# Row sums of squares from half as many matmuls after an add on GpSimd, and the last block in two halves, in a spectral filter with a SwiGLU layer

## The chip, the core and the metric

The kernel runs on one core of a Trainium2 chip. TensorE (PE in the profile) multiplies matrices; VectorE (DVE), ScalarE (ACT) and GpSimd (POOL) do elementwise work, each with its own queue of instructions, worked off in order; SyncE (SP) issues most of the DMA transfers, and GpSimd issues the rest. The metric is the time of one execution on the device, in microseconds.

## What is computed

The input x holds 8 sequences of 3008 rows with 256 channels. Each channel of each sequence is filtered in the frequency domain; every row of the result then goes through an RMS norm and a SwiGLU layer of width 1536.

```
X = rfft(x, axis=1)
y = irfft(X * (filt_r + 1j * filt_i), n=3008, axis=1)      # 8 x 3008 x 256
r = sqrt(mean(y * y, over the 256 channels) + 1e-6)
n = y / r * rms_g
out = (silu(n @ w_gate) * (n @ w_val)) @ w_out
```

The part of interest is the mean of the squares: one number for each of the 24064 rows, over 256 channels.

## The kernel before

The sequences are numbered b = 0 to 7. The layer works through blocks of 512 rows, m = 0 to 5 for each sequence (the last block of an even sequence has three quarters of 128 rows, 384; that of an odd one carries the even one's remaining rows along). The 1536 hidden channels come in JT = 12 slices, jt. One triple (b, m, jt) is an item, and the loop at the end of the program takes one item per slot. For item i it emits, in this order:

- `pre` work planned for the slot (second halves of the filter products, `swap_unit`),
- `gv` (L410): four matmuls of 512 columns, two into `pg` and two into `pv`; ScalarE's silu of `pg` into `sg` (L424); VectorE's product of `pv` and `sg` into `hh` (L425),
- `plan` work (everything else that prepares later blocks and sequences),
- `down` (L428) of item i-2: four matmuls of 256 columns that add to `po0` and `po1` (L437); on the last slice ScalarE copies `po0` and VectorE `po1` into `o3` (L442, L443),
- `late` work (`q_unit`), then, if due, `o_store`: two DMA issues on SyncE, three for the last block of an odd sequence (L452, L456).

`pg` and `pv` have two buffers each; `po0`, `po1` and `mx` have one.

A block is prepared some ten to twenty slots ahead of its first use, in these steps:

- `n_unit`, once for each half of the channels, dh = 0 and 1 (L318): four matmuls into `psn`; ScalarE writes y times the gain (L324) and, a slot later, the squares `sq`, fp16, 128 partitions by 512 rows for each half (`sq_unit`, L330). The partitions are the channels of the half.
- `q_unit` (L339): for every quarter of 128 rows and each half, one matmul with the quarter of `sq` as weights and a column of ones, so that the sums over channels come out as one column per quarter, `psq`. The second half is added in PSUM. VectorE makes `u` = sum/256 + eps (L343), GpSimd `rho` = u to the power -1/2 (L345), and GpSimd issues the DMA that writes it to DRAM (`r_tmp`, L347). `psq` takes one of the two `pg` buffers.
- `rho_load` (L354): SyncE issues a DMA that spreads the block's values over all partitions, `rb`.
- `xn_unit` (L403): GpSimd multiplies y by `rb` into `xn`, the block's operand in `gv`.

The slots are written out by hand. With t = 72(b-1) for sequence b from 2 on, block m's second `n_unit` stands at slot s1 = t + 55 + 8m (in sequence 2, where t is 72, at t + 59 + 8m), its `sq_unit` at s1 + 1, and q_unit, rho_load and xn_unit at s1 + 2, s1 + 6 and s1 + 10. Block m of sequence b is first used at slot 72b + 12m. While these run, the next sequence goes through its filter: `b_unit` (psb, L241 and L247), `swap_unit` (L271, L273), the add on GpSimd (L277), `bi_unit` (psi, L286), with one of each every four slots; `x_load` (L189) is issued on GpSimd's queue, and `z_store`, `t2_load`, `g_store`, `t4_load` on SyncE's. All work planned for one slot is emitted in the order in which it was planned: earlier sequences first, and in a sequence earlier blocks first.

Of the kernel before, what the change touches and what calls it, by code (L numbers as in the profile page):

```python
# [22 lines left out]
B = 8  # L23
DFF = 1536
JT = DFF // P
H = 24
# [96 lines left out]
def kernel(  # L123
# [33 lines left out]
    psO = ctx.enter_context(tc.tile_pool(name="psO", bufs=1, space=bass.MemoryType.PSUM))  # L157
    psM = ctx.enter_context(tc.tile_pool(name="psM", bufs=1, space=bass.MemoryType.PSUM))
# [11 lines left out]
    wo = glob.tile([P, JT, D], FP16)  # L170
    gsb = glob.tile([P, 2], FP32)
    hhs = [glob.tile([P, 512], FP16, name="hh%d" % i) for i in range(4)]
# [4 lines left out]
    st = {b: {"x": {}, "t1": {}, "t2": {}, "s": {}, "t3": {}, "t4": {}, "y": {}, "sq": {},  # L177
              "u": {}, "xn": {}} for b in range(B)}
# [13 lines left out]
    def bank(i, name):  # L192

        pool, tag = ((psM, "mx"), (psG, "pg"), (psV, "pv"), (psB, "mb"), (psO, "po1"), (psO, "po0"))[i]
        return pool.tile([P, 512], FP32, tag=tag, name=name)
# [111 lines left out]
    def nq(b, m):  # L307
        return 3 if (m == 5 and b % 2 == 0) else 4
# [19 lines left out]
    def sq_unit(b, m, dh):  # L328
        w = nq(b, m) * P
        nc.scalar.activation(out=st[b]["sq"][m][:, dh, 0:w], in_=st[b]["sq"].pop((m, dh))[:, 0:w],  # L330
                             func=AXT.Square)

    def q_unit(b, m):
        sq = st[b]["sq"].pop(m)
        ps = bank(1, "psq")
        n = nq(b, m)
        for q in range(n):
            for dh in range(2):
                nc.tensor.matmul(ps[:, q:q + 1], sq[:, dh, ts(q, P)], ones,  # L339
                                 start=(dh == 0), stop=(dh == 1))  # L340
        u = up.tile([P, 4], FP32, tag="u", name="u")
        rho = up.tile([P, 4], FP32, tag="rho", name="rho")
        nc.vector.tensor_scalar(out=u[:, 0:n], in0=ps[:, 0:n], scalar1=1.0 / D, scalar2=1e-6 * Y_SCALE * Y_SCALE,  # L343
                                op0=ALU.mult, op1=ALU.add)
        nc.gpsimd.tensor_tensor(out=rho[:, 0:n], in0=u[:, 0:n], in1=mhalf[:, 0:n], op=ALU.pow)  # L345
        if (b, m) not in by_matmul:
            nc.gpsimd.dma_start(r_d[b, m, 0:n * P].rearrange("(p q) -> p q", q=n), rho[:, 0:n])  # L347
        else:
            st[b]["u"][m] = rho
# [59 lines left out]
    hh_of = {}  # L409
    po_of = {}  # L410
    late_p = {}

    def gv(b, m, jt):
        w = nq(b, m) * P
        xn = st[b]["xn"][m]
        pg = psG.tile([P, 512], FP32, tag="pg", name="pg")
        pv = psV.tile([P, 512], FP32, tag="pv", name="pv")
        for ps, wt in ((pg, wg), (pv, wv)):
            for dt_ in range(2):
                nc.tensor.matmul(ps[:, 0:w], wt[:, dt_, ts(jt, P)], xn[:, dt_, 0:w],  # L420
                                 start=(dt_ == 0), stop=(dt_ == 1))
        sg = hp.tile([P, 512], FP16, tag="sg", name="sg")
        hh = hhs[(6 * JT * b + JT * m + jt) % 4]
        nc.scalar.activation(out=sg[:, 0:w], in_=pg[:, 0:w], func=AXT.Silu)  # L424
        nc.vector.tensor_tensor(out=hh[:, 0:w], in0=pv[:, 0:w], in1=sg[:, 0:w], op=ALU.mult)  # L425
        hh_of[(b, m, jt)] = hh

    def down(b, m, jt):  # L428
        hh = hh_of.pop((b, m, jt))
        if jt == 0:  # L430
            po_of[(b, m)] = [psO.tile([P, 2, D], FP32, tag="po%d" % i, name="po%d" % i)
                             for i in range(2)]
        po = po_of[(b, m)]

        n = nq(b, m)
        for s4 in range(n):
            nc.tensor.matmul(po[s4 // 2][:, s4 % 2, :], hh[:, ts(s4, P)], wo[:, jt, :],  # L437
                             start=(jt == 0 and s4 % 2 == 0),
                             stop=(jt == JT - 1 and (s4 % 2 == 1 or s4 == n - 1)))
        if jt == JT - 1:  # L440
            o3 = late_p["op"].tile([P, 4, D], FP32, tag="o3", name="o3")
            nc.scalar.activation(out=o3[:, 0:2, :], in_=po[0], func=AXT.Copy)  # L442
            nc.vector.tensor_copy(out=o3[:, 2:n, :], in_=po[1][:, 0:n - 2, :])  # L443
            po_of[(b, m)] = o3

    def o_store(b, m):
        o3 = po_of.pop((b, m))
        rows = out[b * N:(b + 1) * N, :].rearrange("(n2 n1) d -> n2 n1 d", n1=N1)
        for h in range(2):
            w = 3 if (m == 5 and (h or b % 2 == 0)) else 4  # L450
            lo = h * H + 4 * m
            nc.sync.dma_start(rows[:, lo:lo + w, :], o3[h * 64:h * 64 + 64, 0:w, :])  # L452
        if m == 5 and b % 2:

            prev = out[(b - 1) * N:b * N, :].rearrange("(n2 n1) d -> n2 n1 d", n1=N1)
            nc.sync.dma_start(prev[:, H - 1, :], o3[64:P, 3, :])  # L456
# [129 lines left out]
    with tc.manual_schedule():  # L586
# [65 lines left out]
        warm_up(2, 0)  # L652
        first = n_first()
        q_unit(0, 0)
        y_first(*first, 0)
        scale_split(0, 0)
# [24 lines left out]
            for name in ("sp", "ssp"):  # L681
                late_p[name] = ctx.enter_context(tc.tile_pool(name=name, bufs=3))

        items = [(b, m, jt) for b in range(B) for m in range(6) for jt in range(JT)]
        pre, plan, late = {}, {}, {}

        def at(slot, fn, *a):
            todo = {q_unit: late, swap_unit: pre}.get(fn, plan).setdefault(slot, [])
            if fn == sq_unit:
                todo.insert(0, (fn, a))  # L690
            else:
                todo.append((fn, a))

        def norm_plan(b, m, s0, s1, r):
            for dh in range(2):
                at((s0, s1)[dh], n_unit, b, m, dh)
                at((s0, s1)[dh] + 1, sq_unit, b, m, dh)
            steps = (q_unit, rho_load, xn_unit)
            if (b, m) in by_matmul:
                steps = (q_unit, scale_split, scale_apply)  # L700
            for d, fn in zip(r, steps):
                at(s1 + d, fn, b, m, *((3,) if fn == scale_apply else ()))

        for j in range(6, 12):
            at(j - 6, t2_unit, j, 1, 1)
        norm_plan(0, 1, 0, 2, (2, 4, 6))
        at(6, open_late)
        at(20, open_sp)
        for m, s0 in ((2, 4), (3, 15), (4, 19), (5, 23)):
            norm_plan(0, m, s0, s0 + 2, (2, 5, 8))  # L710
        for b in range(1, B):
# [42 lines left out]
            for m in range(6):  # L754
                step = 2 if b == 1 and m < 3 else n_step
                norm_plan(b, m, n_at[m], n_at[m] + step,
                          (2, 6, 10) if b > 1 else (2, 5, 8))

        stores = {}
        for i in range(len(items) + 4):  # L760
            for fn, a in pre.get(i, ()):
                fn(*a)
            if i < len(items):
                gv(*items[i])
            for fn, a in plan.get(i, ()):
                fn(*a)
            if 2 <= i < len(items) + 2:
                down(*items[i - 2])
                if items[i - 2][2] == JT - 1:
                    stores[i + 1] = items[i - 2][:2]  # L770
            for fn, a in late.get(i, ()):
                fn(*a)
            if i in stores:
                o_store(*stores[i])
# [30 lines left out]
```

## Time and profile before

| | |
|---|---|
| time, median of 4 runs | 906.89 us (904.4 to 907.7) |
| the profiled execution | 904.1 us, span 902.3 us, TensorE clock 0.99 |
| GpSimd, s add (L277), 128x512 fp16 | 96 of them, 1152 ns each |
| GpSimd, xn (L403) | 45, 2.80 us on the mean |
| GpSimd, rho (L345) | 48, 1.02 us on the mean |
| VectorE, hh (L425), 512 and 384 columns | 692 and 557 ns |
| ScalarE, sg (L424), 512 and 384 columns | 597 and 492 ns |
| psq matmuls (L339) | 376, with as many weight loads |
| r_tmp, from issue to landing | 1.8 us |
| x load, from issue to landing | 6.3 us |
| output store (L452), two issues | 1.11 us on SyncE, 512 KB |

The page gives, for each engine, busy time, its share of the span and the number of instructions. A group's line gives the line of the program, engine, operation and tiles, the count, busy time and mean length of one, and what ended the idle time ahead of it. The lengths of matmuls are those of one alone; they overlap, so that the distance between starts tells what one costs. A timeline merges neighbouring instructions of one group into a line with a count.

### The profile page before, as it was taken

The numbers are of one execution on the slowest core, as the hardware profiler recorded it, in microseconds if no ns is written. First come the engines' busy times: TensorE is split into PE (matmuls) and PEld (weight loads), VectorE is DVE, ScalarE is ACT, GpSimd is POOL, SyncE is SP. The second block draws the span as 40 slices with busy tenths as digits, with TensorE's granted clock in tenths as the row PEclk, the third lists the DMA queues.
The fourth block names the chain that finished last, engine by engine and source line by source line (L and its number), as shares of the span: only waits on it lengthen the run. The fifth ranks groups of instructions, "written<-read, shape, count | busy, mean of one in ns | idle before, by whom it ended". The sixth has DMA issues, their size and how long they took to land.

```text
span 902.3 us, 17520 instructions
## 1 busy us (share of the span) xinstructions
PE 880.3 (98%) x6329; PEld 561.8 (62%) x6329; DVE 677.1 (75%) x1075; ACT 619.5 (69%) x1047; POOL 391.6 (43%) x353
## 2 busy tenths in 40 slices
PE   8799999999999999999999999999999999999997
PEld 5565666666666666766666666666666666666554
DVE  8766767788987787888788886888878887555554
ACT  8667666677777766877667766787657765676443
POOL 8842730555635552465325552265514552043300
PEclk9699999999999999999999999999999999999999
DMA  9495725674564437434554247332252232321201
GB/s 201 83 182 167 155 56 176 158 172 86 154 176 108 98 73 204 106 95 118 136 144 109 88 98 195 83 100 82 77 170 72 64 88 55 99 69 48 60 24 46
DMA packets 79746, 100.91 MB, mean 112 GB/s; under 512 B 8096, under 2 KB 56416, under 8 KB 79276
## 3 DMA queue, kind: packets, MB, share of 16 engines
q1 hardware_dynamic: 69276, 83.45, 33.0%
q0 software_dynamic: 10384, 16.35, 11.2%
q8 instruction: 49, 0.80, 0.4%
q14 instruction: 37, 0.30, 0.1%
HBM read 67.67 MB, written 46.78 MB: 127 GB/s over the span
## 4 chain that ended last, share of the span: by engine, by line
PE 86%; issue 5%; DMA 3%; DVE 3%; ACT 1%; POOL 1%; SPq 0%; POOLq 0%; ACTq 0%; DVEq 0%
PE po L437 25%; PE pg L420 25%; PE pv L420 25%; PE psb L241 3%; PE psi L286 3%; PE psn L318 2%; PE psa L204 2%; DMA fr<-in_filt_r_dram 1%; PE psq L339 1%; DVE o L443 1%; DMA rb<-r_tmp 1%; DMA g_tmp<-t 1%; DVE fr L614 1%; ACT sg L424 0%; DVE hh L425 0%
## 5 line engine op out<-in xcount | busy, mean ns | idle before, releaser
L425 DVE TENSOR_TENSOR hh<-pv,sg 128x512 f16<-128x512 f32 (+1 forms) x576 | 391.5, 680 | 203.6 <-ACT sg L424 88.8
L424 ACT ACTIVATE sg<-pg 128x512 f16<-128x512 f32 (+1 forms) x576 | 338.9, 588 | 230.8 <-PE pg L420 222.9
L437 PE MATMUL po<-wo,hh 128*128 128x256 f16 x2256 | 342.2, 272 | 2.3 <-DVE o L443 1.6
L420 PE MATMUL pv<-xn,wv 128*128 128x512 f16 (+1 forms) x1152 | 337.9, 375 | 0.0
L420 PE MATMUL pg<-xn,wg 128*128 128x512 f16 (+1 forms) x1152 | 337.8, 375 | 0.0
L437 PEld LDWEIGHTS <-hh 128*128 128x128 f16 x2256 | 216.5, 98 | 99.2 <-issue 3.6
L277 POOL TENSOR_TENSOR s<-s,s 128x512 f16<-128x512 f16 x96 | 110.6, 1152 | 285.4 <-DVE s L271 207.3
L420 PEld LDWEIGHTS <-wv 128*128 128x128 f16 x1152 | 112.6, 98 | 131.3 <-issue 0.6
L403 POOL TENSOR_TENSOR xn<-y,rb 128x1024 f16<-128x1024 f32 (+1 forms) x45 | 126.0, 2799 | 45.5 <-DMA rb<-r_tmp 32.1
L420 PEld LDWEIGHTS <-wg 128*128 128x128 f16 x1152 | 109.1, 98 | 12.3 <-issue 0.3
L345 POOL TENSOR_TENSOR rho<-u,mhalf 128x4 f32<-128x4 f32 (+1 forms) x48 | 48.9, 1019 | 84.8 <-DVE u L343 84.8
L291 ACT ACTIVATE t<-psi 96x512 f16<-96x512 f32 x112 | 66.4, 593 | 12.3 <-PE psi L286 6.4
L324 ACT ACTIVATE y<-psn,gsb 128x512 f32<-128x512 f32 (+1 forms) x94 | 63.8, 679 | 9.7 <-PE psn L318 2.6
L271 DVE TENSOR_TENSOR s<-psb,fi 64x512 f16<-64x512 f32 x96 | 65.7, 685 | 3.0
L273 DVE SCALAR_TENSOR_TENSOR s<-psb,fi 64x512 f16<-64x512 f32 x96 | 66.5, 693 | 1.3
L247 DVE TENSOR_TENSOR s<-psb,fr 128x512 f16<-128x512 f32 x96 | 65.4, 681 | 0.0
L330 ACT ACTIVATE sq<-psn 128x512 f16<-128x512 f32 (+1 forms) x94 | 54.7, 582 | 0.0
L209 ACT ACTIVATE t<-psa 128x512 f16<-128x512 f32 x70 | 41.8, 597 | 5.6 <-PE psa L204 2.4
L286 PE MATMUL psi<-s,wi 128*128 128x256 f16 x248 | 45.4, 273 | 0.0
L241 PE MATMUL psb<-t,wb 96*128 96x256 f16 x224 | 43.0, 272 | 1.2 <-DVE s L264 0.9
L286 PEld LDWEIGHTS <-wi 128*128 128x128 f16 x248 | 24.2, 98 | 27.1 <-issue 2.0
L318 PEld LDWEIGHTS <-t 128*128 128x128 f16 x368 | 28.3, 98 | 19.9
(97 smaller groups left out, 519.1 us busy)
## 6 DMA issues: line engine op xcount, KB each, us to landing
out_dram<-o SPq DMA_DIRECT2D x84, 256.0 KB
xc<-in_x_dram POOLq DMA_DIRECT2D x56, 192.0 KB, 6.3
z_tmp<-t SPq DMA_DIRECT2D x28, 384.0 KB
t<-z_tmp SPq DMA_DIRECT2D x28, 384.0 KB
g_tmp<-t SPq DMA_DIRECT2D x56, 192.0 KB
rb<-r_tmp SPq DMA_DIRECT2D x41, 256.0 KB
t<-g_tmp SPq DMA_DIRECT2D x21, 384.0 KB
out_dram<-o SPq DMA_DIRECT2D x12, 192.0 KB
```

The lines of the kernel that those rows point to most:

```text
L241: nc.tensor.matmul(ps[:, u, :], w[:, k, :], t, start=True, stop=True)
L247: nc.vector.tensor_tensor(out=s1, in0=ps, in1=f1, op=ALU.mult)
L271: nc.vector.tensor_tensor(out=s2[a], in0=ps[e], in1=f2[e], op=ALU.mult)
L273: nc.vector.scalar_tensor_tensor(out=s2[a], in0=ps[e], scalar=-1.0, in1=f2[e], op0=ALU.mult, op1=ALU.mult)
L277: nc.gpsimd.tensor_tensor(out=s, in0=s1, in1=s2, op=ALU.add)
L286: nc.tensor.matmul(ps[:, u, :], wi_at(q, 2 * i + u), ss[q][:, u, :], start=(q == 0), stop=(q == n - 1))
L291: nc.scalar.activation(out=st[b]["t3"][c][:, 2 * r:2 * r + 2, :], in_=ps[0:KR], func=AXT.Copy)
L403: nc.gpsimd.tensor_tensor(out=xv, in0=yv, in1=rv.unsqueeze(1).to_broadcast([P, 2, n, P]), op=ALU.mult)
L420: nc.tensor.matmul(ps[:, 0:w], wt[:, dt_, ts(jt, P)], xn[:, dt_, 0:w], start=(dt_ == 0), stop=(dt_ == 1))
L424: nc.scalar.activation(out=sg[:, 0:w], in_=pg[:, 0:w], func=AXT.Silu)
L425: nc.vector.tensor_tensor(out=hh[:, 0:w], in0=pv[:, 0:w], in1=sg[:, 0:w], op=ALU.mult)
L437: nc.tensor.matmul(po[s4 // 2][:, s4 % 2, :], hh[:, ts(s4, P)], wo[:, jt, :], start=(jt == 0 and s4 % 2 == 0), stop=(jt == JT - 1 and (s4 ...
```

## The change

There are two parts. In the first, for blocks 2 to 5 of sequence 2 and all blocks of sequences 3 to 7, `fold_unit` on GpSimd adds the two halves of `sq` in place, at slot s1 + 2, and `q_unit` multiplies by the ones once per quarter. For these blocks q_unit, rho_load and xn_unit stand at s1 + 4, s1 + 8 and s1 + 11.

In the second, the last block of the last sequence (b = 7, m = 5) is cut into two parts of 256 rows with 12 items each. The first part adds up in `po0`, the second in `po1` and `mx`, one quarter in each. ScalarE and VectorE copy one quarter each. The stores of the second part are two issues on SyncE and one on ScalarE's queue; those of the first are two on SyncE.

```diff
+    def halved(b, m):
+        return b > 2 or (b == 2 and m > 1)
+
+    def fold_unit(b, m):
+        sq, w = st[b]["sq"][m], nq(b, m) * P
+        nc.gpsimd.tensor_tensor(out=sq[:, 0, 0:w], in0=sq[:, 0, 0:w], in1=sq[:, 1, 0:w], op=ALU.add)
+
     def q_unit(b, m):
...
+        parts = 1 if halved(b, m) else 2
         for q in range(n):
-            for dh in range(2):
+            for dh in range(parts):
                 nc.tensor.matmul(ps[:, q:q + 1], sq[:, dh, ts(q, P)], ones,
-                                 start=(dh == 0), stop=(dh == 1))
+                                 start=(dh == 0), stop=(dh == parts - 1))
...
+    def cut(b, m, part):
+        return (0, nq(b, m)) if part is None else (2 * part, 2)
+
-    def gv(b, m, jt):
-        w = nq(b, m) * P
-        xn = st[b]["xn"][m]
+    def gv(b, m, jt, part):
+        q0, n = cut(b, m, part)
+        w = n * P
+        xn = st[b]["xn"][m][:, :, q0 * P:q0 * P + w]
...
+    def down(b, m, jt, part):
+        hh = hh_of.pop((b, m, jt, part))
         if jt == 0:
...
+            where = {None: ((psO, "po0"), (psO, "po1")), 0: ((psO, "po0"),), 1: ((psO, "po1"), (psM, "mx"))}
...
+        per = 1 if part else 2
         for s4 in range(n):
+            nc.tensor.matmul(po[s4 // per][:, s4 % per, :], hh[:, ts(s4, P)], wo[:, jt, :],
+                             start=(jt == 0 and s4 % per == 0),
+                             stop=(jt == JT - 1 and (s4 % per == per - 1 or s4 == n - 1)))
...
+            else:
+                nc.scalar.activation(out=o3[:, 0, :], in_=po[0][:, 0, :], func=AXT.Copy)
+                nc.vector.tensor_copy(out=o3[:, 1, :], in_=po[part][:, 1 - part, :])
...
+    def o_store(b, m, part):
...
+        if part is not None:
+            lo = 4 * m + 2 * part
+            for h, eng in ((1, nc.sync), (0, nc.scalar if part else nc.sync)):
+                w = 2 - h * part
+                eng.dma_start(rows[:, h * H + lo:h * H + lo + w, :], o3[h * 64:h * 64 + 64, 0:w, :])
+            if part:
+                prev = out[(b - 1) * N:b * N, :].rearrange("(n2 n1) d -> n2 n1 d", n1=N1)
+                nc.sync.dma_start(prev[:, H - 1, :], o3[64:P, 1, :])
+            return
...
-        items = [(b, m, jt) for b in range(B) for m in range(6) for jt in range(JT)]
+        items = [(b, m, jt, part) for b in range(B) for m in range(6)
+                 for part in ((0, 1) if (b, m) == (B - 1, 5) else (None,)) for jt in range(JT)]
...
             steps = (q_unit, rho_load, xn_unit)
+            if halved(b, m):
+                at(s1 + 2, fold_unit, b, m)
+                r = (4, 8, 11)
```

More of the change, by code (lines that the diff above doesn't have):

```diff
@@ L419, in gv @@
             for dt_ in range(2):
-                nc.tensor.matmul(ps[:, 0:w], wt[:, dt_, ts(jt, P)], xn[:, dt_, 0:w],
+                nc.tensor.matmul(ps[:, 0:w], wt[:, dt_, ts(jt, P)], xn[:, dt_, :],
                                  start=(dt_ == 0), stop=(dt_ == 1))
         sg = hp.tile([P, 512], FP16, tag="sg", name="sg")
-        hh = hhs[(6 * JT * b + JT * m + jt) % 4]
+        hh = hhs[(6 * JT * b + JT * (m + (part or 0)) + jt) % 4]
         nc.scalar.activation(out=sg[:, 0:w], in_=pg[:, 0:w], func=AXT.Silu)
@@ L425, in gv @@
         nc.vector.tensor_tensor(out=hh[:, 0:w], in0=pv[:, 0:w], in1=sg[:, 0:w], op=ALU.mult)
-        hh_of[(b, m, jt)] = hh
-    def down(b, m, jt):
-        hh = hh_of.pop((b, m, jt))
+        hh_of[(b, m, jt, part)] = hh
+    def down(b, m, jt, part):
+        hh = hh_of.pop((b, m, jt, part))
         if jt == 0:
[L431 to L435, printed above, removed]
+            where = {None: ((psO, "po0"), (psO, "po1")), 0: ((psO, "po0"),), 1: ((psO, "po1"), (psM, "mx"))}
+            po_of[(b, m, part)] = [pool.tile([P, 2, D], FP32, tag=tag, name=tag)
+                                   for pool, tag in where[part]]
+        po = po_of[(b, m, part)]
+        n = cut(b, m, part)[1]
+        per = 1 if part else 2
@@ L436, in down @@
         for s4 in range(n):
-            nc.tensor.matmul(po[s4 // 2][:, s4 % 2, :], hh[:, ts(s4, P)], wo[:, jt, :],
-                             start=(jt == 0 and s4 % 2 == 0),
-                             stop=(jt == JT - 1 and (s4 % 2 == 1 or s4 == n - 1)))
+            nc.tensor.matmul(po[s4 // per][:, s4 % per, :], hh[:, ts(s4, P)], wo[:, jt, :],
+                             start=(jt == 0 and s4 % per == 0),
+                             stop=(jt == JT - 1 and (s4 % per == per - 1 or s4 == n - 1)))
@@ L440, in down @@
         if jt == JT - 1:
             o3 = late_p["op"].tile([P, 4, D], FP32, tag="o3", name="o3")
[L442 to L447, printed above, removed]
-        rows = out[b * N:(b + 1) * N, :].rearrange("(n2 n1) d -> n2 n1 d", n1=N1)
+            if part is None:
+                nc.scalar.activation(out=o3[:, 0:2, :], in_=po[0], func=AXT.Copy)
+                nc.vector.tensor_copy(out=o3[:, 2:n, :], in_=po[1][:, 0:n - 2, :])
+            else:
+                nc.scalar.activation(out=o3[:, 0, :], in_=po[0][:, 0, :], func=AXT.Copy)
+                nc.vector.tensor_copy(out=o3[:, 1, :], in_=po[part][:, 1 - part, :])
@@ new lines, in down @@
+            po_of[(b, m, part)] = o3
+    def o_store(b, m, part):
+        o3 = po_of.pop((b, m, part))
+        rows = out[b * N:(b + 1) * N, :].rearrange("(n2 n1) d -> n2 n1 d", n1=N1)
+        if part is not None:
[7 more added lines that the diff above has]
+            return
@@ L769 @@
                 if items[i - 2][2] == JT - 1:
-                    stores[i + 1] = items[i - 2][:2]
+                    stores[i + 1] = items[i - 2][:2] + items[i - 2][3:]
             for fn, a in late.get(i, ()):
```

## The prediction, made before the changed kernel ran

> **What bounds the kernel now.** I read the page first (busy shares), then TensorE's own waits, then the timeline. Columns of a timeline line: start in us, length, engine, line, operation and tiles, and in brackets the idle time ahead of it and what ended it.
>
> ```profile
> span 902.3 us, 17520 instructions
> PE 880.3 (98%) x6329; PEld 561.8 (62%) x6329; DVE 677.1 (75%) x1075; ACT 619.5 (69%) x1047; POOL 391.6 (43%) x353
> ```
> ```profile
> PE psi L286 <- POOL s L277: 1.7, 1, 1.7
> PE po L437 <- DVE o L443: 1.6, 4, 0.7
> ```
> TensorE is busy 98% of the span. The two lines are the longest of its waits (us in all, times, longest); all of them together are under 15 us. The chain of waits gives TensorE 86%. So TensorE time taken out of sequences 2 to 7 comes off the span unless a new wait takes its place, and GpSimd (43%) has room. But GpSimd and SyncE run their queues in order, so their order has to be walked through.
>
> **Part 1, the row sums: what goes.** "Halved" are blocks 2 to 5 of sequence 2 and all of 3 to 7: 34 blocks. One weight load and one one-column matmul go per quarter of 128 rows: 4 per block, 3 in the last block of sequences 2, 4 and 6, so 34 x 4 - 3 = 133 pairs.
>
> ```profile
> 409.65 0.59 ACT L330 ACTIVATE sq<-psn 128x512 f16<-128x512 f32 x1
> 410.10 1.15 POOL L277 TENSOR_TENSOR s<-s,s 128x512 f16<-128x512 f16 x1 [4.71 <-DVE s L271]
> 411.21 2.87 POOL L403 TENSOR_TENSOR xn<-y,rb 128x1024 f16<-128x1024 f32 x1
> 411.34 0.34 PE L339 MATMUL psq<-ones,sq 128*128 128x1 f16 x8
> 411.55 0.59 PE L420 MATMUL pg<-xn,wg 128*128 128x512 f16 x2
> ...
> 530.49 0.29 PE L339 MATMUL psq<-ones,sq 128*128 128x1 f16 x6
> 530.65 0.59 PE L420 MATMUL pg<-xn,wg 128*128 128x512 f16 x2
> ```
> The price is not the 163 ns that the row gives one psq matmul: they overlap. Eight hold TensorE from 411.34 to 411.55 (0.21 us), six from 530.49 to 530.65 (0.16): 0.025 us per pair. 133 x 0.025 = **3.3 us saved**. The Trainium skill (TensorE: Matmul & The Clock Gate, Back-to-back issue gap) budgets about 81 ns per matmul for a real stream of weight load and matmul with 128 columns; by that 10.8 us would go. This trace measures the very pairs, so 0.025 stands.
>
> **What comes: the adds.** 34 GpSimd adds. The nearest row is the s add (L277), the same 128x512 f16 form: 1.15 us, 39 us in all, on an engine that idles over 500. A rule speaks against it: the skill (GPSIMD Engine Reference, Engine selection) gives an elementwise add to VectorE, since GpSimd needs about twice as long for two inputs. The rows show that ratio (1.15 us against 0.68 for VectorE's 128x512 products), but not that it costs: by the rule VectorE would get 34 x 0.68 = 23 us in slots where it already has two products of 0.69 in 1.3 to 1.7 us; on GpSimd the longer add costs nothing as long as it ends before TensorE asks for the sum. Could it slow VectorE from the side? The hh product takes 692 ns on the mean from 600 to 660 us, beside busy GpSimd, and 692 from 850 to 895, with GpSimd idle. If each add did hold one product up, 34 x 0.69 = 23 us of VectorE time would be late, much of it in slack; I take 0.
>
> **The order on GpSimd.** I number slots by item (12 per block). With eight slots per block (12 us here), the old order is: s add, xn of the block before, rho and its DMA issue, x loads if any, s add. The new one puts the add (slot s1+2) ahead of that xn and rho two slots later. From the lines above: s add to 411.25, the new add to 412.4, xn to 415.3. The psq matmuls, now at the end of slot s1+4, come at about 414.7, so the sum is 2.3 us early. rho then ends near 416.4, its issue near 417.3, and the s add at 417.06 slips to about 417.5; its reader psi is six slots (9 us) on. The loop xn, rho, r_tmp, rb, xn takes 10.2 us (790.62 to 800.77) against 12 us a period: it fits. In sequences 3 and 4 the x load of one slot now precedes that slot's r_tmp on GpSimd's DMA queue (block 4); an x load lands after 6.3 us, so xn could be 3 to 4 us late there, 22 slots before its use: hidden. VectorE's u moves to a slot with one more product: 0.16 us against 1.2 us of slack (pv has two buffers).
>
> **One place is not covered.** Sequence 2 changes steps at block 2: block 1's xn keeps the old distance (s1+10), which is the very slot of block 2's add, and was planned first.
>
> ```profile
> 289.48 2.87 POOL L403 TENSOR_TENSOR xn<-y,rb 128x1024 f16<-128x1024 f32 x1
> 292.32 1.03 POOL L345 TENSOR_TENSOR rho<-u,mhalf 128x4 f32<-128x4 f32 x1
> ```
> The add takes rho's place at 292.32 and ends at 293.47; with about 0.15 for the semaphore and the weight load, psq can start at 293.6. TensorE reaches it at 292.87 (the pg start 293.07 less the old psq's 0.2). **+0.7 us**, once.
>
> **The order on SyncE.** rho_load moves two slots back: in every sequence, blocks 0 and 3 now find the output store between, and block 0 has the least time before its use. Shortest is sequence 7, whose preceding block is three quarters wide:
>
> ```profile
> 786.75 0.33 SPq L354 DMA_DIRECT2D rb<-r_tmp  x1
> 789.10 1.11 SPq L452 DMA_DIRECT2D out_dram<-o  x2
> 790.62 2.87 POOL L403 TENSOR_TENSOR xn<-y,rb 128x1024 f16<-128x1024 f32 x1 [5.15 <-DMA rb<-r_tmp]
> 798.86 0.59 PE L420 MATMUL pg<-xn,wg 128*128 128x512 f16 x2
> ```
> psq moves from 782.72 to about 785.5, rho's write lands near 789.6, and the store holds SyncE until 790.2. rb needed 3.87 us from issue to use (786.75 to 790.62); add 0.5 because the store's 512 KB move until about 792.4 by the DMA view: 794.7. xn ends at 797.6, first needed at about 798.65. Margin 1.1 us; in sequences 3 and 5, by the same walk, 2.5 and 2.7; in 4 and 6, with full blocks before, over 6. Cost 0, and up to 1 if I am short.
>
> **Part 2, the last block in halves.** TensorE's work is the same: 256 columns cost 0.109 us (po: four in 0.44), so a half item of four such and two po is 0.65 us against 1.30. ScalarE's silu is 597 ns at 512 columns and 492 at 384, so 387 at 256; VectorE's product 692, 557, so 422: both below 0.65. First wait of the block: po0 from ScalarE's copy instead of po1 from VectorE's, about 0.2 us either way. The end:
>
> ```profile
> 896.64 0.60 ACT L442 ACTIVATE o<-po 128x512 f32<-128x512 f32 x1 [1.21 <-PE po L437]
> 896.86 0.69 DVE L443 COPY o<-po 128x512 f32<-128x512 f32 x1 [0.70 <-PE po L437]
> 897.62 1.11 SPq L452 DMA_DIRECT2D out_dram<-o  x2
> 898.77 0.61 SPq L456 DMA_DIRECT2D out_dram<-o  x1
> ```
> Before: last pg ends at 894.81, silu, product, four po, copy until 897.55. After: behind the last pg less remains (0.22 pv and three times 0.22 po, against 0.43 and three times 0.44), so it ends 0.88 later, at 895.69. Then 0.02 + 0.39 + 0.02 + 0.42 + 0.05, two po 0.38, 0.03, copy 0.415 (the 128x256 row): 897.41. **0.14 saved.** Then the stores: three issues on SyncE in a row, and 512 KB that move from 898.65 to about 901.05. After, 256 KB are left; SyncE issues two, ScalarE one beside them. First data about 1.0 us after the issue (so it is above), at the 215 GB/s of now: 898.45 to 899.7, the last issue (897.95) no later. **1.3 saved**; low end 0.6 (only one issue spared), or -0.5 if ScalarE's first DMA starts a us late, which no row shows; high end 1.6. I take 1.2.
>
> **Sum**: -3.3 + 0.7 - 0.14 - 1.2 = -3.9 us. The profiled execution took 904.1 (span 902.3 and 1.8 around it), so 900.2; it lies 2.8 below the median of the four runs, three of which are at 906.3 to 907.7. Against the median 906.9: **903.0**.
>
> **The cases.**
> - Forecast, 62%: 903.0; own range 901 to 905 (tail 0.5 us either way, one hidden wait exposed, runs spread by 1 to 2).
> - The tail pays nothing because the ScalarE queue's first store starts late, 14%: -3.3 + 0.7 + 0.5 = -2.1, so 904.8. For it: no DMA of ScalarE is in the trace. Against it: fewer bytes and one issue fewer.
> - The pairs are free already, 12%: nothing saved, +0.7, tail -1.3: 906.3. For it: weight loads are pulled ahead of running matmuls. Against it: 0.21 against 0.16 us for eight against six.
> - Slower, 12%: rb behind the output store. If the store's whole 2.3 us and its completion hold rb back, so that it lands 4 us later than I have it, the first xn of sequences 7, 3 and 5 is late by 2.9, 1.5 and 1.3, and that of 4 and 6 is not: 5.7 us, 908.7 in place of 903.0. It decides from rb landing about 3.5 us later than my 794.7 (2.4 + 1.0 + 0.8 = 4.2 us). For it: SyncE stands 199 us in front of stores in all. Against it: the loads are of one ring, in order, and only 512 KB lie ahead.
>
> A measurement of this kernel can't tell under about 0.3% (2.7 us) from no change: faster means below 904.2, slower above 909.6 by the median. The forecast is faster at 0.87, the tail case at 0.4, the free pairs at 0.05: 0.54 + 0.06 + 0.01 = 0.61. Slower is the rb case at 0.45, with 0.06 for waits I have not seen: 0.11. Same: 0.28. Range 900.0 to 907.5: it reaches past the tail and the free-pairs cases and leaves out most of the rb case.
>
> **What would show it.** After: psq groups of four some 0.10 us ahead of the next pg; TensorE waiting about 0.7 us for the new add once, near 293 us, and for nothing else new; the first xn of sequence 7 ending by 797.6 less what was saved before; last data 1.3 us nearer the last copy. It is wrong if TensorE waits for the add in every block, if pg waits for xn at a sequence's start, or if VectorE's products grow beyond 692 ns.

## The result, and the profile after

| | before | after |
|---|---|---|
| median | 906.04 us (903.72 to 909.84, 58 runs) | 902.67 us (900.56 to 907.03, 39 runs) |
| ratio, with its 95% interval | | 0.9964 [0.9957, 0.9971] |
| the profiled execution | 904.1 us, span 902.3 | 906.6 us, span 904.8 |

The changed kernel is faster by 0.36%, or 3.3 us (2.6 to 3.9 by the interval). The forecast was 903.0. The one profiled execution of the changed kernel says the opposite, 2.5 us more, so the first task is to see where in the trace that comes from. These are its first lines, with the span, and busy time, share and instructions of each engine:

```profile
span 904.8 us, 17407 instructions
PE 878.6 (97%) x6244; PEld 563.3 (62%) x6244; DVE 678.8 (75%) x1088; ACT 621.3 (69%) x1060; POOL 430.2 (48%) x387
```

GpSimd has 38.6 us more work (391.6 before), and TensorE is still the bound. The number of matmuls here falls by only 85 although 133 are gone and 48 came with the halves: -133 + 48 = -85.

To compare two traces, I take fixed events in each: ScalarE's copy of `po0` at the end of every block (L442 before, L457 after). The copy of block 5 of sequence 1 is the last one ahead of the change; that of block 3 of sequence 7 is the last one before the cut block plays a part. They split every trace into a start, a middle and an end:

```
us                               before   after   difference
start to copy of (1, 5)          283.5    288.9     +5.4
copy of (1, 5) to copy of (7, 3) 582.94   580.53    -2.41
copy of (7, 3) to the end         35.85    35.33    -0.52
```

(A span is printed to 0.1 us, so the last stretch is good to about 0.05.)

All that is longer lies in the start, where both programs are the same, and nearly all of it in two blocks: (0, 2) takes 2.5 us more and (1, 0) 2.1. In the first of them TensorE waits 2.7 us once for ScalarE's v (L261), and 0.3 in the kernel before. In the eleven traces of this study the start takes from 283.5 to 289.5 us, without order by kernel, while the distance of two copies in the rest agrees to 0.01 us between runs wherever the programs agree and nothing waits for a DMA. So the span of one profile can't tell a change of 3 us here, and the middle and the end can: -2.9 us, inside the interval of the timed runs. From here on I compare these two stretches.

The timeline of the changed kernel where the prediction showed 409.65 to 411.55 of the old one (start, length, engine, line, operation, idle time ahead and what ended it):

```profile
403.37 1.15 POOL L277 TENSOR_TENSOR s<-s,s 128x512 f16<-128x512 f16 x1 [0.46 <-DVE s L271]
404.49 1.16 POOL L338 TENSOR_TENSOR sq<-sq 128x512 f16<-128x512 f16 x1
...
406.95 2.88 POOL L411 TENSOR_TENSOR xn<-y,rb 128x1024 f16<-128x1024 f32 x1 [1.31 <-DMA rb<-r_tmp]
...
407.88 0.24 PE L347 MATMUL psq<-ones,sq 128*128 128x1 f16 x4
407.98 0.59 PE L432 MATMUL pg<-xn,wg 128*128 128x512 f16 x2
...
409.80 1.03 POOL L353 TENSOR_TENSOR rho<-u,mhalf 128x4 f32<-128x4 f32 x1
```

Four psq matmuls hold TensorE for 0.10 us (407.88 to 407.98), where eight held it 0.21. The new add (L338) follows the s add at once, as forecast, and ends 2.2 us before psq needs it. TensorE's waits in the steady part, from 270 us on (us in all, times, longest), show only one for an add:

```profile
PE po L451 <- DVE hh L437: 0.5, 1, 0.5
PE psq L347 <- POOL sq L338: 0.5, 1, 0.5
PE po L451 <- DVE o L458: 0.3, 1, 0.3
```

The wait for the add is the one at block 2 of sequence 2:

```profile
294.90 2.88 POOL L411 TENSOR_TENSOR xn<-y,rb 128x1024 f16<-128x1024 f32 x1
297.75 1.14 POOL L338 TENSOR_TENSOR sq<-sq 128x512 f16<-128x512 f16 x1
298.94 0.17 PEld L347 LDWEIGHTS <-sq 128*128 128x128 f16 x4 [0.76 <-POOL sq L338]
298.95 0.25 PE L347 MATMUL psq<-ones,sq 128*128 128x1 f16 x4 [0.48 <-POOL sq L338]
```

The add stands behind the 2.88 us of block 1's xn, and TensorE loses 0.48 us. No pg waits for xn anywhere. At the start of sequence 7, the place with the least cover, the SyncE queue and GpSimd read:

```profile
792.36 1.11 SPq L479 DMA_DIRECT2D out_dram<-o  x2
...
793.58 0.54 SPq L362 DMA_DIRECT2D rb<-r_tmp  x1
...
798.18 2.87 POOL L411 TENSOR_TENSOR xn<-y,rb 128x1024 f16<-128x1024 f32 x1 [1.79 <-DMA rb<-r_tmp]
```

Behind the output store, rb needs 4.6 us from its issue to xn (3.87 before). xn ends at 801.05, and the block's first matmul starts at 802.03: 1.0 us to spare. The end of the program:

```profile
898.58 0.42 DVE L437 TENSOR_TENSOR hh<-pv,sg 128x256 f16<-128x256 f32 x1 [0.23 <-ACT sg L436]
...
898.82 0.38 ACT L436 ACTIVATE sg<-pg 128x256 f16<-128x256 f32 x1 [0.27 <-PE pg L432]
...
899.46 0.42 DVE L437 TENSOR_TENSOR hh<-pv,sg 128x256 f16<-128x256 f32 x1 [0.46 <-ACT sg L436]
...
900.37 0.42 DVE L461 COPY o<-mx 128x256 f32<-128x256 f32 x1 [0.49 <-PE mx L451]
900.67 0.47 SPq L471 DMA_DIRECT2D out_dram<-o  x1
900.88 0.55 ACTq L471 DMA_DIRECT2D out_dram<-o  x1
901.23 0.55 SPq L474 DMA_DIRECT2D out_dram<-o  x1
```

From the end of the last copy (900.79) to the end of the span it is 4.01 us, against 4.75 before. The three issues now overlap in part. One thing is odd: the last product hh starts 0.26 us after the end of its silu (899.20), while the one ahead starts 0.03 after (898.55 to 898.58).

### The profile page after: what moved, and what is told of

Same layout as the page of the kernel before. It is cut to its first block, busy times and chain, and to the rows that moved or that the text cites. A ratio compares the mean times of both kernels' runs of the same rounds, so it can differ in the third digit from the quotient of the medians.

```text
span 904.8 us, 17407 instructions
## 1 busy us (share of the span) xinstructions
PE 878.6 (97%) x6244; PEld 563.3 (62%) x6244; DVE 678.8 (75%) x1088; ACT 621.3 (69%) x1060; POOL 430.2 (48%) x387
## 4 chain that ended last, share of the span: by engine, by line
PE 84%; issue 5%; DMA 4%; DVE 3%; ACT 2%; POOL 1%; POOLq 0%; ACTq 0%; SPq 0%
PE po L451 25%; PE pg L432 25%; PE pv L432 24%; PE psi L286 3%; PE psb L241 3%; PE psn L318 2%; DMA fr<-in_filt_r_dram 2%; PE psa L204 2%; DMA g_tmp<-t 1%; DMA rb<-r_tmp 1%; DVE o L458 1%; DVE fr L641 1%; PE psq L347 1%; DVE hh L437 1%; ACT sg L436 0%
## 5 line engine op out<-in xcount | busy, mean ns | idle before, releaser
L437 DVE TENSOR_TENSOR hh<-pv,sg 128x512 f16<-128x512 f32 (+2 forms) x588 | 393.3, 670 | 204.0 <-ACT sg L436 91.9
L436 ACT ACTIVATE sg<-pg 128x512 f16<-128x512 f32 (+2 forms) x588 | 340.8, 580 | 227.9 <-PE pg L432 217.9
L432 PE MATMUL pg<-xn,wg 128*128 128x512 f16 (+2 forms) x1176 | 340.3, 371 | 0.0
L432 PE MATMUL pv<-xn,wv 128*128 128x512 f16 (+2 forms) x1176 | 340.0, 371 | 0.0
L432 PEld LDWEIGHTS <-wv 128*128 128x128 f16 x1176 | 115.0, 98 | 129.4 <-issue 1.2
L432 PEld LDWEIGHTS <-wg 128*128 128x128 f16 x1176 | 111.5, 98 | 12.7 <-issue 0.3
L338 POOL TENSOR_TENSOR sq<-sq 128x512 f16<-128x512 f16 (+1 forms) x34 | 38.5, 1131 | 32.6 <-ACT sq L330 32.6
```

## The experiments

The theory: the pairs pay 0.025 us each and nothing else in the steady part changes, apart from the one wait; the end pays for fewer bytes and one issue fewer. The rivals are those of the prediction: the pairs cost nothing anyway, the end pays nothing, the loads of rb have no cover. Each run below was timed beside the kernel before (a ratio with its 95% interval), apart from the last one, which was only profiled. The stretches are those of the table above.

```
us               middle    end   time, median   ratio [95%]
before           582.94   35.85
after            580.53   35.33     902.67      0.9964 [0.9957, 0.9971]
sums alone       580.82   35.87     905.10      0.9971 [0.9953, 0.9988]
halves alone     582.93   35.35     906.57      0.9983 [0.9967, 0.9999]
idle adds        583.73   35.84     907.34      1.0005 [0.9987, 1.0023]
two queues       582.94   35.87     907.51      0.9995 [0.9979, 1.0011]
add first        579.88   35.32     903.69      0.9974 [0.9956, 0.9992]
one queue        580.72   35.74     903.61      0.9977 [0.9963, 0.9991]
two stores       579.88   35.08     903.38      0.9966 [0.9951, 0.9981]
steps late       585.00   35.35     908.80      1.0027 [1.0014, 1.0041]
one bank         580.53   35.73
```

The kernel before had a median of 907.4 beside the first four of these and 906.2 beside the next four, so medians are compared through the ratios only. Those of the experiments are 2.4 to 3.3 us wide. They fit the sums of the two stretches throughout but don't settle differences under 2 us; the stretches do.

**The sums alone.** The last block stays whole:

```diff
-                 for part in ((0, 1) if (b, m) == (B - 1, 5) else (None,)) for jt in range(JT)]
+                 for part in (None,) for jt in range(JT)]
```

> The adds on GpSimd and the halved row sums alone, the last block whole as before. Theory (the pairs are what is saved): 133 pairs at 0.025 us less one wait for the add, so from the psq of slot 141 to the first pg of the last block 2.4 us less than before (599.8 in place of 602.2), the end as before; 2.4 to 2.7 us faster, ratio about 0.997. Rival (the two parts lean on each other, or the pairs were free): no difference from before within 0.5 us.

Middle -2.12, end as before (35.87). The pairs are not free. The wait for the add is longer here than in the changed kernel, though both have the same program in that place:

```profile
295.77 2.87 POOL L411 TENSOR_TENSOR xn<-y,rb 128x1024 f16<-128x1024 f32 x1 [0.25 <-DMA rb<-r_tmp]
...
299.81 0.25 PE L347 MATMUL psq<-ones,sq 128*128 128x1 f16 x4 [0.77 <-POOL sq L338]
```

Ahead of the add, xn itself waited 0.25 us for its rb. So the price of this wait hangs on when a DMA lands: 0.48 to 0.77 for TensorE in the traces that have this add behind this xn, and 0.65 to 0.95 for the block as a whole.

**The halves alone.** No block is halved in its sums:

```diff
-        return b > 2 or (b == 2 and m > 1)
+        return False
```

> The last block in halves and the two queues alone, the row sums as before. Theory (the end is a fixed time after the last store's issue): from the first pg of the last block to the end of the span 22.1 us in place of 22.6, so 0.5 us faster, ratio about 0.9994. Rival (the prediction: bytes set the end): 1.3 us faster, ratio 0.9985.

Middle as before (582.93), end -0.50. The two parts don't touch each other: -2.12 for the sums and -0.50 for the halves make the -2.93 of both together but for 0.3, by which the wait for the add was longer with the sums alone. The rival in which the end pays nothing is out.

**The adds without the saving.** GpSimd does an operation of the same size at the same place (the second half of the squares times one), all steps stand in their new slots, and TensorE keeps eight matmuls per block:

```diff
-        nc.gpsimd.tensor_tensor(out=sq[:, 0, 0:w], in0=sq[:, 0, 0:w], in1=sq[:, 1, 0:w], op=ALU.add)
+        nc.gpsimd.tensor_tensor(out=sq[:, 1, 0:w], in0=sq[:, 1, 0:w], in1=ones.to_broadcast([P, w]), op=ALU.mult)
...
-        parts = 1 if halved(b, m) else 2
+        parts = 2
```

(with the last block whole)

> As the row sums alone, but GpSimd's operation multiplies the second half of sq by one, so nothing is summed, and TensorE does all eight psq matmuls at the moved slots. Theory (adds and moved steps cost one wait in sequence 2 and else nothing): 0.5 to 0.7 us slower than before, ratio 1.0006, and each block keeps its old length. Rival (adds or moved steps cost something in every block, which the pairs more than pay): 1.5 us or more slower.

Middle +0.79. The distance of neighbouring copies, less the same in the kernel before, says where. This is a selection of the blocks from sequence 2 on:

```
us, to the copy of   after   sums alone   idle adds   add first   steps late
b=2 m=0              +0.55     +0.84        +0.52       -0.10       -0.10
b=2 m=5              -0.11     -0.10         0.00       -0.11       +1.37
b=4 m=4              -0.10     -0.10         0.00       -0.10       -0.20
b=4 m=5              -0.10     -0.10         0.00       -0.10       +1.57
b=6 m=5              -0.10     -0.10         0.00       -0.10       +2.18
b=7 m=0              -0.14     -0.14        +0.06       -0.14       -0.24
b=7 m=2              +0.10     +0.10        +0.21       +0.10       +0.10
```

With idle adds, all the blocks but three are unchanged to 0.01 us: 34 operations of 1.04 us on GpSimd (the adds take 1.15) and three moved steps cost nothing there. The three are the wait for the add (+0.52) and two places in sequence 7 (+0.06, +0.21). The sums alone against idle adds gives the price of the pairs: 583.73 - 580.82 = 2.91, and the wait was 0.42 longer with the sums alone (0.84 - 0.52, and 0.10 for that block's saved pairs, which its 0.84 has in it): 3.33 us, or 0.025 for each of 133.

The place in sequence 7, block 2, is a wait that had been hidden. In the kernel before:

```profile
834.61 0.34 PE L339 MATMUL psq<-ones,sq 128*128 128x1 f16 x8
834.81 0.59 PE L420 MATMUL pg<-xn,wg 128*128 128x512 f16 x2
835.24 0.59 PE L420 MATMUL pv<-xn,wv 128*128 128x512 f16 x2
835.67 0.84 PE L437 MATMUL po<-wo,hh 128*128 128x256 f16 x4
```

and in the changed kernel:

```profile
838.39 0.38 PE L451 MATMUL po<-wo,hh 128*128 128x256 f16 x2
839.06 0.38 PE L451 MATMUL po<-wo,hh 128*128 128x256 f16 x2 [0.28 <-DVE o L458]
```

At a block's start the third po waits until VectorE has copied `po1` out. Before, eight psq matmuls stood just ahead of this and took 0.2 us of time that TensorE had to wait anyway (the four po then last 0.84 instead of 0.60). Moved two slots on, they leave the wait bare: 0.2 us are given back, twice what this block's own pairs save (+0.10 in the table). The +0.06 of block 0 is the same wait, shorter since VectorE's copy of the three-quarter block ahead takes 0.41 us and not 0.68.

That no other block does this comes from the next sequence's filter. In sequences 2 to 6 psq stood just behind a copy nine times too, but four matmuls of the filter lie there between pv and po, as in the kernel before at sequence 3:

```profile
423.49 0.34 PE L339 MATMUL psq<-ones,sq 128*128 128x1 f16 x8
...
424.55 0.38 PE L286 MATMUL psi<-s,wi 128*128 128x256 f16 x2
424.77 0.38 PE L241 MATMUL psb<-t,wb 96*128 96x256 f16 x2
424.99 0.60 PE L437 MATMUL po<-wo,hh 128*128 128x256 f16 x4
```

These 0.44 us cover the copy without psq. Sequence 7 has no sequence behind it, and so no such matmuls.

**The add ahead of block 1's xn.** Block 1's xn goes one slot later; nothing else is changed:

```diff
-                           (2, 6, 10) if b > 1 else (2, 5, 8))
+                           (2, 6, 11 if (b, m) == (2, 1) else 10) if b > 1 else (2, 5, 8))
```

> The changed kernel with one step moved: the xn of block 1 of sequence 2 is planned one slot later, so that the add of block 2 is ahead of it on GpSimd. From ScalarE's output copy of the last block of sequence 1 to that of block 3 of sequence 7 (called the middle): before 582.94 us, the changed kernel 580.53. If the one wait for the add (0.48 us in the trace, with what stands around it +0.55 for that block) is a loss of its own, the middle is 580.0 and the block of the wait gives -0.10 like all others. If the wait only took up time that TensorE would have lost to the next engine anyway, it comes back behind the add and the middle stays at 580.5. The end is that of the changed kernel (35.33 from the copy of block 3 to the end).

```profile
291.37 1.16 POOL L338 TENSOR_TENSOR sq<-sq 128x512 f16<-128x512 f16 x1
292.49 2.88 POOL L411 TENSOR_TENSOR xn<-y,rb 128x1024 f16<-128x1024 f32 x1
294.77 0.24 PE L347 MATMUL psq<-ones,sq 128*128 128x1 f16 x4
```

The wait is gone, the block gives -0.10 like the others, and the middle is 579.88: 0.65 less. The wait was a loss of its own, and nothing behind it took it up.

**The second queue without the halves.** The kernel before, with the second of its last three stores on ScalarE's queue:

```diff
-            nc.sync.dma_start(rows[:, lo:lo + w, :], o3[h * 64:h * 64 + 64, 0:w, :])
+            eng = nc.scalar if (b == B - 1 and m == 5 and h) else nc.sync
+            eng.dma_start(rows[:, lo:lo + w, :], o3[h * 64:h * 64 + 64, 0:w, :])
```

> The kernel before, with one change: of the last block's three stores the second one is issued on ScalarE's queue. All 512 KB still move at the end. Theory (the end comes about 3.55 us after the last issue starts): the last issue starts 0.55 us sooner, and the span ends 0.5 us sooner after the last copy (4.2 in place of 4.75). Rival (bytes at 215 GB/s set the end): unchanged, 4.75.

The expectation missed. The issues came closer together and the end (35.87) did not move:

```profile
902.05 0.69 DVE L458 COPY o<-po 128x512 f32<-128x512 f32 x1 [0.71 <-PE po L451]
902.80 0.47 SPq L480 DMA_DIRECT2D out_dram<-o  x1
902.83 0.56 ACTq L480 DMA_DIRECT2D out_dram<-o  x1
903.32 0.59 SPq L484 DMA_DIRECT2D out_dram<-o  x1
```

The last issue starts 0.58 us after the last copy (902.74), before 1.22 after; the end comes 4.76 after, before 4.75. With 512 KB in flight the issues are not what the end waits for. So I formed a second theory, that the end is the later of two things, the last issue with 3.55 us behind it or the last byte with 1.3 behind it, and tested it on the halves.

**One queue for the halves.**

```diff
-            for h, eng in ((1, nc.sync), (0, nc.scalar if part else nc.sync)):
+            for h, eng in ((1, nc.sync), (0, nc.sync)):
```

> The changed kernel with the third store of the last half block issued on SyncE instead of ScalarE's queue: three issues of about 0.55 us in a row. Theory: the end is the later of two, 3.55 us after the start of the last issue, or 1.3 us after the last byte; with 256 KB left in two halves the last issue decides. Then the last issue starts 0.5 to 0.6 us later and the end from the copy of block 3 of sequence 7 is 35.85 instead of 35.33, so that the halves alone bring nothing and the second queue all of the 0.5. Rival: the bytes decide (half the bytes, 215 GB/s), the second queue brings nothing, and the end stays at 35.33. Middle 580.5 by both.

End 35.74: the last issue is later by 0.60 (1.04 us after the last copy instead of 0.44), and the end by 0.41. So the halves with one queue bring 0.1 us over the kernel before (35.85), and the second queue the other 0.4. The middle is 580.72 because the wait for the add was 0.66 in this trace.

**Two stores, and a step ahead of the store.** One issue on each queue (the one on SyncE now writes two rows that lie apart), rho_load one slot earlier, and block 1's xn a slot later as in the run with the add first:

```diff
-                r = (4, 8, 11)
+                r = (4, 7, 11)
```

```diff
+                row = b * N + H + lo
+                if not (h and part):
+                    dst = rows[:, h * H + lo:h * H + lo + 2, :]
+                else:
+                    dst = bass.AP(tensor=out.tensor, offset=out.offset + row * D,
+                                  ap=[[N1 * D, 64], [((b - 1) * N + H - 1 - row) * D, 2], [1, D]])
+                eng.dma_start(dst, o3[h * 64:h * 64 + 64, 0:2, :])
```

> The changed kernel with block 1's xn a slot later as in the run before, rho_load one slot earlier (ahead of the output store of that slot on SyncE), and the last half block stored by one issue on SyncE and one on ScalarE's queue instead of two and one. Theory (last issue decides): the last issue starts 0.35 us sooner, the end is 34.95 to 35.0 from the copy of block 3 of sequence 7. Rival (bytes decide): 35.3. The earlier rho_load should bring no time (xn was never waited for), only a shorter wait of GpSimd for rb: the middle is 580.0 if the add's wait is a loss of its own, 580.5 if not. Sum by the theory: 0.9 us under the changed kernel.

```profile
895.21 0.42 DVE L461 COPY o<-mx 128x256 f32<-128x256 f32 x1 [0.49 <-PE mx L451]
895.70 0.65 SPq L476 DMA_DIRECT2D out_dram<-o  x1
895.73 0.58 ACTq L476 DMA_DIRECT2D out_dram<-o  x1
```

The last issue starts 0.10 us after the last copy (895.63), 0.34 sooner than in the changed kernel, and the end is 35.08: 0.25 sooner, between the theory and its rival (the table of the ends below says why). The middle is that of the run with the add first alone (579.88), so the earlier rho_load brings no time, as expected. Middle and end together are 0.90 us under the changed kernel. The timed runs, 0.9966 against 0.9964 with intervals of 0.003 and 0.0014, don't tell the two apart.

**All steps four slots late.** This measures how much cover there is for the first xn of a sequence:

```diff
-                r = (4, 8, 11)
+                r = (8, 12, 15)
```

> The changed kernel with q_unit, rho_load and xn_unit of the halved blocks four slots later each (s1 + 8, 12, 15), to measure how much cover the first xn of a sequence has. Theory, by the walk of the prediction with the measured times (in sequence 7 the first xn ended 1.0 us before the first matmul that needs it; four slots are 5 to 6 us, of which the steps of half a period already counted leave about 3): TensorE waits about 2 us for xn at the start of sequence 7 and about 1 us each at sequences 3 and 5, while the wait for the add in sequence 2 goes (-0.5): the middle is 3.5 us over the changed kernel's 580.53. Rival: the cover is longer than the walk says (another block's matmuls stand between), and the middle is 580.0. A pg that waits for xn in the trace, or none, decides.

```profile
385.80 0.59 PE L432 MATMUL pg<-xn,wg 128*128 128x512 f16 x2 [1.23 <-POOL xn L411]
...
596.40 0.59 PE L432 MATMUL pg<-xn,wg 128*128 128x512 f16 x2 [1.43 <-POOL xn L411]
...
801.61 0.59 PE L432 MATMUL pg<-xn,wg 128*128 128x512 f16 x2 [2.05 <-POOL xn L411]
```

These three lines of the timeline stand at the starts of sequences 3, 5 and 7. Those are the three places that the prediction named, with the longest wait at the one it named first, sequence 7, and no other pg waits. The middle is 4.47 over the changed kernel's: the three waits, 4.7 us, a little around them, and less the wait for the add (0.65), which is gone here too. The estimate had been 3.5, since I had the first two at 1 us. So the rival with rb behind the store had the right place. What it got wrong was the price: in the changed kernel rb took 0.7 us longer from its issue than before, where the forecast had 0.5 and the rival needed about 4 us on top of that.

**Both quarters in one bank.** The last part adds both quarters in `po1`, as the first part does in `po0`:

```diff
-            where = {None: ((psO, "po0"), (psO, "po1")), 0: ((psO, "po0"),), 1: ((psO, "po1"), (psM, "mx"))}
+            where = {None: ((psO, "po0"), (psO, "po1")), 0: ((psO, "po0"),), 1: ((psO, "po1"),)}
...
-        per = 1 if part else 2
+        per = 2
...
-                nc.vector.tensor_copy(out=o3[:, 1, :], in_=po[part][:, 1 - part, :])
+                nc.vector.tensor_copy(out=o3[:, 1, :], in_=po[0][:, 1, :])
```

> The changed kernel with both quarters of the second part of the last block added up in po1 (as the first part does in po0), instead of one in po1 and one in mx. It is about VectorE's last product hh, which starts 0.26 us after the end of its silu (899.20 to 899.46), where all the others start 0.03 after it, and about the block's length from its first pg to the last copy (18.08 us, forecast 17.73). If the late product comes from the second accumulation in mx, the product starts 0.2 us earlier and the end lies 35.1 us after the copy of block 3 of sequence 7 instead of 35.33. If it doesn't, the product stays 0.26 late, and the end at 35.33, or up to 0.1 later, since the copy on ScalarE can't start before both quarters are done (now 0.11 apart). Middle 580.5 to 580.8 by both.

```profile
896.97 0.38 ACT L460 ACTIVATE o<-po 128x256 f32<-128x256 f32 x1 [1.17 <-PE po L451]
...
897.38 0.42 DVE L461 COPY o<-po 128x256 f32<-128x256 f32 x1 [0.90 <-ACT o L460]
```

The late product stays (0.26 us here too), so it does not come from `mx`. But both expectations missed the end, 35.73: VectorE's copy waits for ScalarE's when both read one bank. In the changed kernel they start 0.11 us apart, here 0.41. The Trainium skill (PSUM — Partial Sum Buffer, PSUM bank collisions raise a hardware error) says that two engines must not read one bank at the same time and that software has to keep them apart. The trace agrees that the program does so: VectorE's copy waits for a semaphore of ScalarE's. This is what that order costs where it counts; what would happen without it, no run shows. So the second part pays only with both, the second queue and the second accumulator in `mx`: without either, 0.1 us of its 0.5 is left.

## Why the prediction was right

```
us                                    forecast   measured   by
133 pairs                              -3.3       -3.33     sums alone against idle adds
wait for the add, sequence 2           +0.7       +0.65     add first against after
two places in sequence 7                0         +0.27     idle adds, +0.06 and +0.21
last block, first pg to last copy      -0.14      +0.21     traces
last copy to the end                   -1.2       -0.74     traces
sum                                    -3.9       -2.94
```

The timed difference is 3.3 us with an interval of 2.6 to 3.9, which holds the measured sum and, at its edge, the forecast one. Sign and mechanism are those of the forecast. That its 903.0 lies within 0.4 us of the measured 902.67 is in part luck: it started from a median of 906.9 of four runs, and the 58 runs have 906.04, so two errors partly cancel (from 906.04, the forecast sum gives 902.1). Three of its steps were measured one by one:

- **The pairs.** 0.025 us each. The starts in the trace gave the price; the 163 ns that the group has as its mean would have been wrong, and so would the 81 ns that the Trainium skill (TensorE: Matmul & The Clock Gate, Back-to-back issue gap) states for pairs whose matmul has 128 columns: by those the middle would have lost 10.8 us. The prediction set that figure against matmuls of one column (128x1 in the lines); for up to 64 columns the same section states a floor of about 25 ns from start to start, and this trace agrees: 0.025 us, the weight load included.
- **The wait.** The order of the plan put the add behind a 2.88 us xn in one block, and the walk through GpSimd's queue found it with 0.7 us. The trace has 0.48 for TensorE and the block as a whole 0.65. How near this is to the forecast is chance too, since other traces have up to 0.95.
- **What was costed at nothing.** GpSimd's 38.5 us of adds, the moved rho and its DMA, the product hh (692 ns as before from 600 to 660 us) and SyncE's new order cost nothing, with a margin for xn in sequence 7 of 1.0 us where 1.1 was forecast. The late steps show that this margin is real and that it ends where the walk said. What the forecast did not see is the price of moving psq away from a wait, 0.27 us in sequence 7.

The term that was mis-sized is the end: -0.53 instead of -1.34 from the last block's first pg on. It has two parts.

The block itself is 0.35 us longer than worked out. 0.24 of this is the last product, which starts 0.26 after its silu where I had 0.02. What it waits for stays open: neither the profile's own reading (the silu) nor `mx` is the cause. In every trace with the halves it starts within 0.01 us of the end of the fourth po or mx matmul ahead of it, though it reads nothing that they write; no run tried whether it waits for them.

The rest is behind the last copy. The table sets the last issue, the last byte (the last 0.1 us slice of the DMA view that has data) and the end against the last copy's end. Its last column counts the semaphore waits with which SyncE closes the program, from that of the store that lands last on:

```
us after the last copy   last issue   last byte   end    end less last byte   waits
before                      1.22         3.4      4.75         1.4              2
two queues                  0.58         3.4      4.76         1.4              2
after                       0.44         2.3      4.01         1.7              8
one queue                   1.04         2.7      4.43         1.7              8
two stores                  0.10         2.5      3.77         1.3              1
one bank                    0.14         2.3      4.00         1.7              8
```

The forecast had the last byte 2.29 us after the copy, and it came at 2.3: bytes and rate were right. Wrong was the step from there: 1.25 us, read from the kernel before (1.36 by the packets of its trace) and taken as a constant. It is 1.70 in the changed kernel.

The traces show what it consists of. SyncE ends with one wait for each of the eight semaphores that the transfers of SyncE and ScalarE take in turn. The order is the same in all eleven traces, each wait takes 0.06 us once there is nothing left to land, and from the last of them it is 0.84 us to the end in every trace. The wait for the store that lands last is over 0.36 to 0.42 us after the last byte. SyncE's semaphore instructions from there on, before, after and with two stores (two of each line belong to the closing 0.84 us):

```profile
L800 SPq EVENT_SEMAPHORE  x4: 17/22/28, 901.4 to 902.3; - x4
...
L831 SPq EVENT_SEMAPHORE  x10: 17/28/28, 903.5 to 904.7; - x10
...
L833 SPq EVENT_SEMAPHORE  x3: 17/17/28, 898.5 to 899.3; - x3
```

Before, the last store's semaphore is the last but one of the list. The halves have two stores more, which moves it to the first place, so that seven waits still follow: 0.37 + 8 x 0.06 + 0.84 = 1.7 us, against 0.39 + 2 x 0.06 + 0.84 = 1.4. This is an accident of the number of stores, and it took 0.34 us from the gain.

The last byte and this list account for all six rows. Two queues leave the last byte where it was. One queue delays it by 0.41 us, and the end by the same 0.41. One bank has the last issue 0.30 sooner, and neither the last byte nor the end moves. With two stores the last byte is 0.2 later, but the list is 0.44 shorter, and the end comes 0.25 sooner. So my second theory (the last issue and 3.55 us, or the last byte and 1.3) is wrong: with one bank it gives 3.7, and the end is at 4.0.

## What to carry to other kernels

Price a short matmul by the distance of starts in the row where it stands, and ask of each place whether it stood in front of a wait: there it was free, and moving it lays the wait bare. Moving a step in a hand-written order is safe where a walk through each queue leaves a margin; the walk has to include the one block where the old and the new distances meet. The time behind the last byte is no constant of the kernel: look in the trace where the last store stands in the closing list of waits. When a change is worth 3 us and the start of the program wanders by 6, compare stretches between two fixed events of the trace, and not the spans.

## What the runs showed of the hardware

- A pair of a 128x128 weight load and a one-column matmul costs TensorE 0.025 us between matmuls of 512 columns (133 pairs, 3.33 us).
- 34 operations of 128x512 fp16 on GpSimd beside busy VectorE and ScalarE cost these nothing that 0.01 us per block would show (idle adds, 1.04 us each).
- Two copies from one PSUM bank, which the program puts one after the other, start 0.41 us apart, against 0.11 from two banks (one bank).
- From the last byte of the last store to the end it is 1.3 to 1.7 us: 0.36 to 0.42 until SyncE's wait for it is over, 0.06 for each wait in the closing list from it on, and 0.84 that is the same in all eleven traces.
- The first 284 to 290 us, the same program in all, vary by 6 us from trace to trace, and the rest by 0.01 us per block where nothing waits for a DMA. TensorE's granted clock over the first 50 us was 0.84 in the trace of before, 0.81 in that of after and 0.86 in that with the slowest start (sums alone), so its mean does not explain the starts; why the waits in the two blocks named above differ was not looked into.
